# Routed attention and a SiLU layer: a relisted opening, output quarters in any free bank, and one-hot codes scaled on GpSimd and turned by transposing transfers

## The chip, the cores and the metric

The kernel runs on one core of a Trainium2 chip. The core has a matrix engine (TensorE, PE in the profile), a vector engine (VectorE, DVE), an activation engine (ScalarE, ACT), GpSimd (POOL) and SyncE (SP), which here does nothing but issue transfers. Each engine works off its own instructions in order and waits at one until the semaphores that it needs have come. The metric is device time of one execution in microseconds (us); less is better.

## The reference

Four batches of eight heads, 768 tokens, 64 numbers a head. Queries and keys are assigned to the nearest of 16 centroids of their head (by cosine), and a query attends only to the keys of its own cluster. The result passes through a layer with SiLU.

```python
q_assign = np.argmax(np.einsum('bhsd,hcd->bhsc', q_n, c_n), axis=-1)
k_assign = np.argmax(np.einsum('bhsd,hcd->bhsc', k_n, c_n), axis=-1)
mask = q_assign[:, :, :, None] == k_assign[:, :, None, :]
scores = np.where(mask, scale * np.matmul(q, k.transpose(0, 1, 3, 2)), -1000000000.0)
attn = softmax(scores)                      # over the keys
x = matmul(attn, v), heads side by side     # 3072 x 512
h = x @ w_in                                # 3072 x 2048
out = (h * sigmoid(h)) @ w_out              # 3072 x 512, float32
```

## The kernel before

**Masking by matmul.** The mask is not computed as such. Queries and keys lie transposed in a tile `ab` (128 partitions: 64 of the high half of each number in f16, 64 more that at first hold the low halves). The low halves serve the logits against the centroids; then 16 of their partitions (64 to 79) are overwritten with the one-hot code of the row's cluster, scaled by 16384 (`OHV`) and, for keys, shifted by -16384, so that one score matmul gives the product plus 0 for rows of one cluster and a large negative number otherwise. The exponential then does the masking.

**Jobs.** One job prepares one head of one batch: `load` (two transfers on SP's queue, into `raw`, eight buffers), `hi` and `lo` (scale to f16 and the rest, into `hl`), the transpose into `ab` (by PE and an evacuation for batch 0: `tr`, `ev`; by a transposing transfer on SP for the others: `xpose`), `logits`, then on DVE the sum `lsum`, the maximum `mx_n`, and the comparison `ge_n` that writes the one-hot code. The code then has to be turned: `cd_mm` does it with two PE matmuls against the identity, into the right half of a PSUM bank (`psC`), `cd_ev` scales and shifts it on DVE on its way to SBUF (`cd`), and a transfer on SP puts it on partitions 64 to 79 of `ab`. Batch 0 has jobs 0 to 7 for keys and half the queries, and `x0`, `x1` for the other queries of four heads each.

**Steps.** The main work is 192 steps; a step is the scores of one head against two of six key tiles for half of the queries (`qk_mm`: two matmuls of 384 columns into one of two buffers `pS`), and their exponential on ACT (`exp`, 768 columns). Three steps make a head's half. Step 7 + 6n holds attention times v for two heads (`pv`: 36 small matmuls), followed by the normalisation on DVE (`norm`) and a transpose into `xt`, on PE for batch 0 and the last pair, by a transposing transfer (`xn_d`) for the rest. When four such pairs of a half are done, 5 steps later, the half's feed-forward work may start: 16 units A (`unit_a`: four matmuls `ph` of 384 columns, tanh on ACT, one product on DVE into `gt`) and then three output tiles B (`part_b`) of four quarters each (four matmuls `po` of 512 columns); the fourth quarter is followed by an evacuation `ot` and a transfer out.

**Order.** Nothing is scheduled by the compiler: the program is written in the order in which each engine has it. The first 24 steps stand in a list of words (`plan`): `hi0.A` is the high half of job 0 on ACT, `lo`, `tr`, `evk`/`evq`, `L`, `mx`, `ge`, `cm`/`ce` the further parts of a job, `xh`, `xl`, `xp`, `xq`, `xu`, `xw` those of `x0` and `x1`, `qk` and `ex` a step, `pa`/`pb`/`pc` a third of `pv`, `nm` a normalisation, `pt`/`pe` the transpose into `xt`, `vl` and `v` load and conversion of a v, `w` a weight load issued by GpSimd, `j` filler matmuls on zeros, `a` and `e` the first unit A. From step 24 on a loop writes the steps; jobs 8 to 31 have their parts put at fixed steps about p = 32 + 3.5h, 64 + 5h and 104 + 5h for the eight heads h of batches 1, 2 and 3. Units A and quarters B fill what the step leaves: `take` gives them out as long as the estimated PE time of the step (T = 1.46) has room.

**Banks.** PSUM has eight banks: four for the two buffers `pS`, banks 0 to 2 handed out by `bank()` as they come free (`free`), and bank 3, which `part_b` uses for every output tile after the opening.

Of the kernel before, what the change touches and what calls it, by code (L numbers as in the profile page):

```python
# [10 lines left out]
f16 = mybir.dt.float16  # L11
# [5 lines left out]
class Job:  # L17


    def __init__(self, name, srcs, groups, uses):  # L20
        self.name = name
        self.srcs = srcs
        self.groups = groups
        self.uses = uses
        self.n = 3 * len(groups)


@with_exitstack
def kernel(
# [10 lines left out]
    nc = tc.nc  # L40
# [47 lines left out]
    pace = const.tile([1, 1], f16, name="pace")  # L88
    kadd = const.tile([128, 2], f32, name="kadd")
    ohm = [const.tile([128, 2 * HC * 6], f16, name=f"om{n}") for n in range(3)]  # L90


    raws, hls, abs_ = {}, {}, {}
# [104 lines left out]
    def ge_n(job):  # L198
        m = (job.n + 1) // 2
        nn[job.name] = len(nn)  # L200
        mx = mxn.pop(job.name)[:, 0 : 2 * m].rearrange("p (h m) -> p h m", h=2)
        nc.vector.tensor_tensor(
            out=ohv(job), in0=Ls.pop(job.name), in1=mx.unsqueeze(2).to_broadcast([128, 2, HC, m]), op=ALU.is_ge
        )

    def cd_mm(job):
# [314 lines left out]
    def first(op, n, eng, banks):  # L521
# [40 lines left out]
        elif op in ("pa", "pb", "pc"):  # L562
            t = "abc".index(op[1])
            pv(2 * n, 0, banks and banks[0], [(t, 0), (t, 1)])
        elif op in ("px", "py"):
            pv(2 * n, 0, banks and banks[0], [(t, "xy".index(op[1])) for t in range(NM)])
        elif op == "a":
            begun[n] = unit_a_begin(0, 0, n)
        elif op == "e":
            unit_a_end(0, 0, n, begun.pop(n) if n in begun else unit_a_begin(0, 0, n))()  # L570
        elif op == "nm":
            norm(2 * n, 0)
        elif op == "pt":
            xn_t(2 * n, 0, banks[0])
        elif op == "pe":
            xn_ev(2 * n, 0, eng)
        elif op == "xr":
# [24 lines left out]
    plan = """  # L602
        hi0.A lo0 tr0.32 hi2.P j2.1 evk0.D evq0.A c5.01 j2.2 stk hi1.A L0.3 lo2 j1.2 kad xr0
        mx0 tr2.02 hi3.P ge0 j1.1 lo1 j1.1 evk2.A evq2.D ct0.10 hi4.P lo3 vl1 vl0 xr1 L2.2 ctq0 ctk0 tr1.31 mx2 hi5.P
        qk0 evk1.D evq1.A vl2 ex0 tr3.01 ge2 lo4 cm2 hi6.P L1.3 evk3.A ce2.D qk1 vl4 evq3.A mx1 tr4.02 ex1 ge1
        L3.1 hi7.P evk4.D evq4.A qk2 mx3 ct1.02 ex2 ge3 v1 lo5 cm3 ctq1 L4.3 v0 ce3.A ctk1 w0 tr5.01 mx4 v2
        qk3 ge4 evk5.A w1 evq5.D qk4 lo6 cm4 ex3 j2.2 ce4.D vl3 ex4 v4 qk5 lo7 L5.2 ex5 qk6 mx5 tr6.10 ex6 ge5 qk7
        xh0.P evk6.D cm5 ex7 qk8 ce5.D tr7.31 evq6.D ex8 qk9 evk7.D L6.2 vl5 ex9 w2 evq7.D qk10 mx6 v3 L7.0 ex10
        ge6 qk11 cm6 ex11 pa0.3 ce6.D pb0 mx7 qk12 w3 ge7 ex12 v5 qk13 pc0 cm7 ex13 nm0 ce7.D qk14 ex14 xl0 xh1.P qk15 xp0.1 pt0.3 qk16 pe0.D xu0.D xq0.2 xw0.D
        ex15 vl6 w4 ex16 qk17 pa1.0 vl7 xL0.2 qk18 pb1 ex17 w5 xM0 xm0 xg0 qk19 pc1 xc0 ex18 nm1 xe0.D qk20 w6 v6 pa2.1 ex19  # L610
        pt1.0 qk21 pb2 ex20 pe1.D xl1 w7 v7 qk22 pc2 xp1.2 ex21 nm2 xu1.D qk23 xq1.0 px3.3 ex22 pt2.1 xw1.D ex23 w8 pe2.D xL1.2 xM1 xm1 xg1 a0 py3 nm3 xc1 a1 w9 pt3.3 pe3.D xe1.D e0 e1 qk24 ex24 e2
    """.split()
    for word in plan:
        name, *rest = word.split(".")
# [17 lines left out]

    for n in range(10, 12):
        put(25 + 2 * (n - 10), w_load, n, 24 + 2 * (n - 10))
    for i in range(H, B * H):
        b, h = divmod(i, H)
        p = int((32 + 3.5 * h, 64 + 5 * h, 104 + 5 * h)[b - 1]) | 1
        job = jobs[i]
        e = 1 if b == 1 else 2
        put(p - 8 - 2 * (b > 1), load, job)  # L640
        put(p - 6, load_v, i)
        put(p - 3 * e, hi, job)
        put(p - 1 - e, lo, job)
        put(p - e, xpose, job)
# [16 lines left out]
    def take(hold, held):  # L661
# [156 lines left out]
```

## Time and profile before

| what | value |
|---|---|
| time, median of 3 runs | 324.86 us (323.74 to 325.95) |
| the profiled execution: its time / its span | 326.72 us / 324.9 us |
| mean granted clock of TensorE | 0.989 |
| read from / written to main memory | 27.30 MB / 6.29 MB |

The span runs from the first to the last instruction. Shares of busy time are means over stages that differ: the opening with its list (to about 45 us), batch 1's jobs beside the first half's feed-forward work, batches 2 and 3, a stretch without jobs (from about 231 us), and the tail. The page's groups give an operation's mean duration and, behind the bar, the time for which its engine stood idle just before it and what ended that. In the timeline the bracket at the end of a row is such a wait. Matmul ends are modelled, and one begins before its predecessor ends, so distances between starts are the better measure.

### The profile page before, as it was taken

What the parts mean: (1) busy time and instruction counts of PE and PEld (TensorE: products, weight loads), DVE (VectorE), ACT (ScalarE), POOL (GpSimd) and SP (SyncE); (2) the same over time, 40 slices, a digit from 0 to 9 for tenths busy, and PEclk for the clock granted to TensorE, in tenths of its full rate; (3) what the DMA queues carried; (4) which work ended last, traced back from release to release, by engine and by line L of the source; (5) the groups of instructions that cost most, each with busy time, mean ns of one, the idle gap of its engine ahead of it and who ended that gap; (6) DMA issues with size and microseconds to landing.
All of it is one profiled execution on the core that took longest, in us unless ns stands there. A gap on an engine that the chain in (4) does not pass through costs nothing.

```text
span 324.9 us, 7844 instructions
## 1 busy us (share of the span) xinstructions
PE 307.2 (95%) x3173; PEld 191.3 (59%) x3173; DVE 211.7 (65%) x445; ACT 209.4 (64%) x332; POOL 41.0 (13%) x68
## 2 busy tenths in 40 slices
PE   6997999997989999999999999999999999999995
PEld 2665765655556555665566656666566556655644
DVE  5897566779778655987598857893456315632641
ACT  2597649766468665885488656985589648961620
POOL 4884331101000000000010002000000000000000
PEclk9899899999999999999999999999999999999999
DMA  7756999999945686677887567853110111011001
GB/s 218 248 108 132 168 148 253 184 241 206 247 120 135 162 184 186 150 161 132 237 186 185 128 171 210 138 115 83 53 46 12 37 54 46 6 42 46 32 32 68
DMA packets 72613, 43.14 MB, mean 133 GB/s; under 512 B 50016, under 2 KB 68608, under 8 KB 72576
## 3 DMA queue, kind: packets, MB, share of 16 engines
q1 hardware_dynamic: 69024, 38.14, 47.3%
q0 software_dynamic: 3264, 4.20, 8.6%
q8 instruction: 25, 0.41, 0.5%
q10 hardware_dynamic: 288, 0.30, 0.3%
q14 instruction: 12, 0.10, 0.1%
HBM read 27.30 MB, written 6.29 MB: 103 GB/s over the span
## 4 chain that ended last, share of the span: by engine, by line
PE 74%; DVE 14%; ACT 3%; DMA 3%; issue 2%; SPq 2%; POOL 0%; DVEq 0%; ACTq 0%
PE po L430 23%; PE ph L380 20%; PE pS L313 13%; PE pO L330 9%; PE psN L168 3%; DVE hl L120 3%; DVE gt L400 2%; ACT tn L399 2%; DVE ot L437 2%; PE phs L410 2%; ACT P L318 2%; DVE mxn L193 2%; DMA ab<-hl 1%; PE po L782 1%; DVE L L180 1%
## 5 line engine op out<-in xcount | busy, mean ns | idle before, releaser
L318 ACT ACTIVATE P<-pS 128x768 f16<-128x768 f32 x192 | 152.6, 811 | 67.2 <-PE pS L313 67.0
L380 PE MATMUL ph<-xt,win_s 128*128 128x384 f16 x480 | 91.2, 326 | 3.2 <-DVE gt L400 1.7
L313 PE MATMUL pS<-ab 128*128 128x384 f16 x384 | 92.2, 328 | 0.7 <-ACT P L318 0.6
L430 PE MATMUL po<-wout_s,gt 128*128 128x512 f16 x368 | 89.2, 379 | 1.6 <-DVE ot L437 0.9
L400 DVE SCALAR_TENSOR_TENSOR gt<-tn,ph 128x384 f16<-128x384 f32 x120 | 64.0, 551 | 24.3 <-ACT tn L399 23.8
L399 ACT ACTIVATE tn<-ph 128x384 f32<-128x384 f32 x120 | 58.8, 496 | 15.9 <-PE ph L380 11.7
L380 PEld LDWEIGHTS <-win_s 128*128 128x128 f16 x480 | 45.8, 98 | 33.3 <-issue 4.7
L430 PEld LDWEIGHTS <-gt 128*128 128x128 f16 x368 | 34.5, 98 | 37.0 <-issue 3.4
L313 PEld LDWEIGHTS <-ab 128*128 128x128 f16 x384 | 34.7, 98 | 25.5 <-issue 1.7
L330 PEld LDWEIGHTS <-P 128*128 128x128 f16 x1152 | 40.3, 98 | 5.3 <-issue 0.7
L330 PE MATMUL pO<-vt,P 128*128 128x65 f16 x1152 | 41.5, 193 | 0.0
L260 POOL CAST vt<-vn 128x384 f16<-128x384 f32 x32 | 17.0, 533 | 157.5 <-DMA vn<-in_v_dram 127.5
L120 DVE SCALAR_TENSOR_TENSOR hl<-raw,hl 128x768 f16<-128x768 f32 (+3 forms) x35 | 33.9, 972 | 0.4 <-POOL hl L113 0.3
L437 DVE TENSOR_SCALAR ot<-po 128x512 f32<-128x512 f32 x23 | 15.8, 689 | 27.5 <-PE po L430 27.1
L168 PEld LDWEIGHTS <-ab 128*128 128x128 f16 x496 | 18.1, 98 | 5.6 <-DMA ab<-hl 1.5
L180 DVE TENSOR_REDUCE L<-psN 128x192 f32<-128x384 f32 x24 | 13.2, 552 | 11.9 <-PE psN L168 11.9
L168 PE MATMUL psN<-stk,ab 128*128 128x32 f16 (+1 forms) x496 | 19.3, 187 | 1.2 <-DMA ab<-hl 1.1
L342 DVE TENSOR_TENSOR xn<-pO,zr 128x384 f16<-128x384 f32 x32 | 17.8, 557 | 1.1
L340 DVE RECIPROCAL zr<-pO 128x6 f32<-128x6 f32 x32 | 6.2, 194 | 15.7 <-PE pO L330 15.7
L224 DVE TENSOR_SCALAR cd<-psC,kadd 96x256 f16<-96x256 f32 x24 | 11.4, 474 | 6.2 <-PE psC L211 6.0
L113 POOL TENSOR_SCALAR hl<-raw 128x576 f16<-128x576 f32 (+1 forms) x8 | 14.4, 1816 | 2.6 <-DMA raw<-in_q_dram 1.7
L115 DVE TENSOR_SCALAR hl<-raw 128x768 f16<-128x768 f32 x24 | 13.4, 560 | 2.0 <-DMA raw<-in_k_dram 1.9
(68 smaller groups left out, 138.8 us busy)
## 6 DMA issues: line engine op xcount, KB each, us to landing
vn<-in_v_dram SPq DMA_DIRECT2D x32, 192.0 KB, 3.1
raw<-in_k_dram SPq DMA_DIRECT2D x31, 192.0 KB, 3.3
out_dram<-ot SPq DMA_DIRECT2D x23, 256.0 KB, 2.3
raw<-in_q_dram SPq DMA_DIRECT2D x24, 192.0 KB, 2.8
win_s<-in_moe_w_in_dram POOLq DMA_DIRECT2D x8, 256.0 KB, 6.3
wout_s<-in_moe_w_out_dram POOLq DMA_DIRECT2D x4, 512.0 KB, 8.7
ab<-cd SPq DMA_DIRECT2D x26, 48.0 KB, 2.3
raw<-in_q_dram SPq DMA_DIRECT2D x2, 384.0 KB, 5.0
```

Of the source, the lines that this page charges most:

```text
L120: nc.vector.scalar_tensor_tensor(out=hl[:, s, 1, :], in0=raws[job.name][:, s, :], scalar=QS, in1=hl[:, s, 0, :], op0=ALU.mult, op1=ALU.sub ...
L168: nc.tensor.matmul(L[:, n % 2, :, n // 2], ab[:, i, :], stk[:, job.groups[i // 3][0], x : x + w], start=(x == 0), stop=(x + w == 2 * HC),)
L260: nc.gpsimd.tensor_copy(vt[:, :, 0:D], vns.pop(i))
L313: nc.tensor.matmul(pS[:, e, 0:HALF], abs_[kj.name][:, kn, :], rhs, start=True, stop=True)
L318: nc.scalar.activation(out=P, in_=pst.pop(u)[:, :, 0:HALF], func=AF.Exp, bias=0.0, scale=ESC)
L330: nc.tensor.matmul(o[:, (2 * t + h) * VW : (2 * t + h + 1) * VW], Ps[i + h, c, j // 2][:, j % 2, ts(t, 128)], vtb[(i + h) % 13][:, j, 0:VW ...
L342: nc.vector.tensor_tensor(out=xn, in0=ov[:, :, 0:D], in1=zr.unsqueeze(2).to_broadcast([128, 2 * NM, D]), op=ALU.mult)
L380: nc.tensor.matmul(ph[:, 0:HALF], win_s[:, r, ts(fb, 128)], xts[b, c][:, r, :], start=(r == 0), stop=(r == NR - 1))
L399: nc.scalar.activation(out=tn, in_=ph[:, 0:HALF], func=AF.Tanh, bias=0.0, scale=0.5)
L400: nc.vector.scalar_tensor_tensor(out=gt[:, fb, :], in0=tn, scalar=1.0, in1=ph[:, 0:HALF], op0=ALU.add, op1=ALU.mult)
L430: nc.tensor.matmul(po, gts[b, c][:, fc, ts(t, 128)], wout_s[:, fc, :], start=(fc == 0), stop=(fc == NFB - 1))
L437: nc.vector.tensor_scalar(out=ot, in0=po, scalar1=0.5, scalar2=None, op0=ALU.mult)
```

## The change

The opening's list is written anew: the weight loads `w0` to `w7` come earlier, `xl0` moves ahead of `ce7` and `nm0`, `xh1` moves back, job 8 is loaded at the end of the list (`r8`), v 6 and 7 are loaded before it, and the first filler has 13 matmuls and not 11. Loads of batches 1 to 3 are issued earlier. A `part_b` that starts while no unit A is left takes a free bank of 0 to 2 if there is one, and the next tile may follow at once. For jobs 16 to 31 the code is compared into a tile `ohd` with the two parts 128 columns apart, GpSimd scales it in place (`c_scale`, two instructions), a transposing transfer on SP turns it (`c_xpose`), and a second transfer, three steps later, moves it to `ab` (`c_move`); the two matmuls and the evacuation fall away for them.

```diff
+        self.late = name[0] == "h" and int(name[1:]) >= 16
+    ohd = [const.tile([128, 2, 128], f16, name=f"od{n}") for n in range(3)]
     def ohv(job):
         m = (job.n + 1) // 2
+        if job.late:
+            return ohd[nn[job.name] % 3][:, :, 0 : HC * m].rearrange("p h (c m) -> p h c m", m=m)
...
+    def c_scale(job):
+        o = ohv(job)
+        nc.gpsimd.tensor_scalar(out=o[:, :, :, 0:3], in0=o[:, :, :, 0:3], scalar1=OHV, scalar2=None, op0=ALU.mult)
+        nc.gpsimd.tensor_scalar(
+            out=o[:, :, :, 3:6], in0=o[:, :, :, 3:6], scalar1=OHV, scalar2=-OHV, op0=ALU.mult, op1=ALU.add
+        )
+    def c_xpose(job):
+        cd = cds[job.name] = mp.tile([128, 2, 128], f16, name="cdt", bufs=2)
+        nc.sync.dma_start_transpose(cd, ohd[nn[job.name] % 3].rearrange("p h n -> p (h n)"))
+    def c_move(job):
+        cd = cds.pop(job.name)
+        nc.sync.dma_start(
+            abs_[job.name][64 : 64 + HC, :, :].rearrange("p n c -> p (n c)"), cd[0 : 6 * HC].rearrange("p h c -> p (h c)")
+        )
...
-    fill(11)
+    fill(13)
...
-        ge6 qk11 cm6 ex11 pa0.3 ce6.D pb0 mx7 qk12 w3 ge7 ex12 v5 qk13 pc0 cm7 ex13 nm0 ce7.D qk14 ex14 xl0 xh1.P qk15 xp0.1 pt0.3 qk16 pe0.D xu0.D xq0.2 xw0.D
-        ex15 vl6 w4 ex16 qk17 pa1.0 vl7 xL0.2 qk18 pb1 ex17 w5 xM0 xm0 xg0 qk19 pc1 xc0 ex18 nm1 xe0.D qk20 w6 v6 pa2.1 ex19
...
+        ge6 qk11 cm6 ex11 pa0.3 ce6.D pb0 mx7 qk12 w7 ge7 ex12 qk13 pc0 cm7 xl0 ex13 ce7.D vl6 vl7 r8 qk14 nm0 ex14 xp0.1 qk15 xu0.D xq0.2
+        ex15 qk16 xw0.D pt0.3 ex16 pa1.0 pe0.D qk17 xL0.2 ex17 xh1.P pb1 qk18 xM0 xm0 xg0 ex18 pc1 qk19 xc0 nm1 xe0.D v6 v7 ex19
...
+    for od in ohd:
+        put(60, nc.gpsimd.memset, od, 0.0)
     for i in range(H, B * H):
...
-        put(p - 8 - 2 * (b > 1), load, job)
-        put(p - 6, load_v, i)
+        if i > H:
+            put(p - (8 + min(h, 4) if b == 1 else 16), load, job)
+        put(p - (6 if b == 1 else 9), load_v, i)
...
-        put(p + 7, cd_mm, job)
-        put(p + 7, cd_ev, job, "D")
+        if job.late:
+            put(p + 6, c_scale, job)
+            put(p + 6, c_xpose, job)
+            put(p + 9, c_move, job)
+        else:
+            put(p + 7, cd_mm, job)
+            put(p + 7, cd_ev, job, "D")
...
-            f = part_b(*qb.pop(0))
+            f = part_b(*qb.pop(0), None if not qa and free else 3)
             if f:
                 late.append(f)
-                gap = -1
+                gap = -1 if qa else 1
```

More of the change, by code (lines that the diff above doesn't have):

```diff
@@ L203, in ge_n @@
             out=ohv(job), in0=Ls.pop(job.name), in1=mx.unsqueeze(2).to_broadcast([128, 2, HC, m]), op=ALU.is_ge
+        )
[5 more added lines that the diff above has]
+        )
+    cds = {}
+    def c_xpose(job):
[5 more added lines that the diff above has]
+            abs_[job.name][64 : 64 + HC, :, :].rearrange("p n c -> p (n c)"), cd[0 : 6 * HC].rearrange("p h c -> p (h c)")
         )
@@ L576, in first @@
             xn_ev(2 * n, 0, eng)
+        elif op == "r":
+            load(jobs[n])
         elif op == "xr":
@@ L603 @@
         hi0.A lo0 tr0.32 hi2.P j2.1 evk0.D evq0.A c5.01 j2.2 stk hi1.A L0.3 lo2 j1.2 kad xr0
[L604 to L608, printed above, removed]
-        ge6 qk11 cm6 ex11 pa0.3 ce6.D pb0 mx7 qk12 w3 ge7 ex12 v5 qk13 pc0 cm7 ex13 nm0 ce7.D qk14 ex14 xl0 xh1.P qk15 xp0.1 pt0.3 qk16 pe0.D xu0.D xq0.2 xw0.D
-        ex15 vl6 w4 ex16 qk17 pa1.0 vl7 xL0.2 qk18 pb1 ex17 w5 xM0 xm0 xg0 qk19 pc1 xc0 ex18 nm1 xe0.D qk20 w6 v6 pa2.1 ex19
-        pt1.0 qk21 pb2 ex20 pe1.D xl1 w7 v7 qk22 pc2 xp1.2 ex21 nm2 xu1.D qk23 xq1.0 px3.3 ex22 pt2.1 xw1.D ex23 w8 pe2.D xL1.2 xM1 xm1 xg1 a0 py3 nm3 xc1 a1 w9 pt3.3 pe3.D xe1.D e0 e1 qk24 ex24 e2
+        mx0 tr2.02 hi3.P ge0 j1.1 lo1 j1.1 evk2.A evq2.D ct0.10 hi4.P lo3 vl1 vl0 xr1 L2.2 ctq0 ctk0 tr1.31 mx2 hi5.P w0
+        qk0 evk1.D evq1.A vl2 ex0 tr3.01 ge2 lo4 cm2 hi6.P w1 L1.3 evk3.A ce2.D qk1 vl4 evq3.A mx1 tr4.02 ex1 ge1
+        L3.1 hi7.P w2 evk4.D evq4.A qk2 mx3 ct1.02 ex2 ge3 v1 lo5 cm3 ctq1 L4.3 v0 w3 ce3.A ctk1 tr5.01 mx4 v2 vl3
+        qk3 ge4 evk5.A evq5.D qk4 lo6 cm4 w4 ex3 j2.2 ce4.D vl5 ex4 v4 qk5 lo7 L5.2 ex5 qk6 mx5 tr6.10 ex6 ge5 qk7
+        xh0.P w5 evk6.D cm5 ex7 qk8 ce5.D tr7.31 evq6.D ex8 qk9 evk7.D L6.2 v3 ex9 w6 evq7.D qk10 mx6 v5 L7.0 ex10
+        ge6 qk11 cm6 ex11 pa0.3 ce6.D pb0 mx7 qk12 w7 ge7 ex12 qk13 pc0 cm7 xl0 ex13 ce7.D vl6 vl7 r8 qk14 nm0 ex14 xp0.1 qk15 xu0.D xq0.2
+        ex15 qk16 xw0.D pt0.3 ex16 pa1.0 pe0.D qk17 xL0.2 ex17 xh1.P pb1 qk18 xM0 xm0 xg0 ex18 pc1 qk19 xc0 nm1 xe0.D v6 v7 ex19
+        pa2.1 qk20 pt1.0 pb2 ex20 pe1.D qk21 pc2 xl1 ex21 nm2 xp1.2 qk22 xu1.D ex22 xq1.0 px3.3 qk23 xw1.D pt2.1 pe2.D ex23 w8 xL1.2 xM1 py3
+        xm1 xg1 nm3 a0 xc1 pt3.3 a1 w9 pe3.D xe1.D e0 e1 qk24 ex24 e2
     """.split()
```

## The prediction

> **What bounds the kernel.** I read the page first, then busy time by stage, then the chain of waits, then the timeline around each gap of TensorE (PE). The profiled execution took 326.72 us, 324.9 of them span; the median of the three timed runs is 324.86. I work out differences on the span and take them off the median; a profiled run of the new kernel should read about 1.9 us higher.
>
> ```profile
> span 324.9 us, 7844 instructions
> PE 307.2 (95%) x3173; PEld 191.3 (59%) x3173; DVE 211.7 (65%) x445; ACT 209.4 (64%) x332; POOL 41.0 (13%) x68
> ```
>
> ```profile
> 7.90:11.30 3.40, 3.40 (x37) 2.02 (x35) 2.03 (x5) 1.50 (x4) 3.40 (x3) 0.51 0.96 304
> 31.90:35.10 3.20, 3.20 (x28) 2.53 (x27) 1.38 (x3) 0.98 (x2) 3.20 (x7) 0.50 0.98 206
> 0.00:45.50 45.50, 39.04 (x574) 27.25 (x575) 32.69 (x91) 27.14 (x40) 26.27 (x40) 0.92 0.75 170
> 45.50:68.70 23.20, 23.20 (x205) 14.04 (x203) 15.76 (x30) 18.48 (x32) 3.35 (x7) 1.00 1.03 217
> 68.70:85.00 16.30, 13.86 (x172) 8.46 (x171) 13.91 (x30) 9.26 (x12) 2.03 (x4) 1.00 1.02 225
> 116.70:231.00 114.30, 112.00 (x1175) 69.74 (x1173) 85.82 (x173) 78.63 (x124) 7.86 (x14) 1.00 0.67 156
> ```
>
> Columns are stage, length, then PE, PE weight load, DVE, ACT, POOL (busy, instructions), granted clock, DMA share. PE sets the pace nearly everywhere; outside the opening and 68.7 to 85 us it hardly idles. So only three things shorten the run: fewer matmuls, fewer gaps, or a full clock in the two stretches where 0.5 was granted. A busy PE is not PE at its peak, so I price matmuls by distances from start to start:
>
> ```profile
> 251.38 0.33 PE pS L313 x2
> 251.71 0.65 PE ph L380 x4
> 252.36 0.86 PE po L430 x4
> ```
>
> That is 0.33 for a step's two score matmuls, 0.65 for an input-projection unit, 0.86 for an output quarter. A step that takes longer than its matmuls at these prices has lost time.
>
> **Opening (to 45.5 us): -3.0.** Two stalls matter, both followed by half clock.
>
> ```profile
> 1.18 4.13 PE L461 MATMUL junk<-zz 128*128 128x512 f16 x11 [1.18 <-DVE zz L471]
> ```
> ```profile
> 6.90 0.51 PE L143 MATMUL pTk<-ident,hl 128*128 128x128 f16 x6 [1.59 <-DVE hl L120]
> ```
> ```profile
> 10.59 0.32 DVE L193 TENSOR_REDUCE mxn<-psN 128x10 f32<-128x160 f32 x1 [0.99 <-PE psN L168]
> ```
> ```profile
> 78.84 0.52 PE L168 MATMUL psN<-stk,ab 128*128 128x32 f16 x12 [1.13 <-DMA ab<-hl]
> ```
>
> Two more filler matmuls take 2 x 4.13/11 = 0.75 and lie inside the 1.59 wait for the low halves, so they cost nothing; were that wait gone, 0.75. They leave PE 0.84 idle instead of 1.59. The gap of 1.13 at 78.84 left the clock at 1.00, so I expect the dip at 7.9 to 11.3 to go. It is worth 0 (DVE and POOL work beside it) to 1.7 (half of 3.4); I take 0.8, near the 0.99 that DVE waits for the half-speed logits.
>
> ```profile
> 27.98 0.33 DVE L202 TENSOR_TENSOR om<-psN,mxn 128x160 f16<-128x160 f32 x1
> ```
> ```profile
> 30.07 2.13 POOL L113 TENSOR_SCALAR hl<-raw 128x768 f16<-128x768 f32 x1
> 30.08 1.63 DVE L120 SCALAR_TENSOR_TENSOR hl<-raw,hl 128x768 f16<-128x768 f32 x1
> ```
> ```profile
> 31.77 0.82 PE L143 MATMUL pTk<-ident,hl 128*128 128x128 f16 x6 [1.43 <-DVE hl L120]
> ```
> ```profile
> 39.00 0.95 DVE L120 SCALAR_TENSOR_TENSOR hl<-raw,hl 128x768 f16<-128x768 f32 x1
> ```
>
> In the old list `xl0` stands behind `nm0` and `ce7`, beside the GpSimd conversion `xh1`, and takes 1.63; PE waits 1.43 for it. In the new list it follows `ge7` (ending 28.3) and `xh1` comes four steps later: 28.3 + 0.95 to 1.63 = 29.3 to 29.9, while PE came to the transposes that need it at 31.77 - 1.43 = 30.34 and will now come some 0.7 earlier, with two scores and a waiting buffer fewer ahead. Of 1.43 I leave 0.3: -1.1. Then the dip at 31.9 should go too, worth 0 to 1.6; since ACT is busy only 0.98 of 3.20 there, PE sets the time, and I take 1.4. The price of the new order is that `nm0` and the evacuations `xu0`, `xw0` come later on DVE, and weight loads w0 to w2 come ahead of conversions on POOL: 0 to 1.0, taken 0.3. Sum -0.8 - 1.1 - 1.4 + 0.3 = -3.0, between -4.6 and 0.
>
> The Trainium skill ("TensorE: Matmul & The Clock Gate", Part 1) says the clock halves after an idle window of about 3.4 us, a free-running one. The two half-clock stretches are about that long, but each follows only 1.4 to 1.6 us of idle in one piece, so the trace shows a lower threshold; by the page's rule alone neither edit would touch the clock (a rival below).
>
> **Middle (batch 1 jobs, 45.5 to 116.7): -1.3.** Loads go up to four steps earlier on SP's queue, job 8's load goes into the opening. Where DMA is full (share 1.03, 1.02), this moves load traffic and removes none.
>
> ```profile
> 74.33 2.13 SPq L129 DMA_TRANSPOSE ab<-hl  x1
> ```
> ```profile
> 122.46 2.75 PE L430 MATMUL po<-wout_s,gt 128*128 128x512 f16 x12 [0.87 <-DVE ot L437]
> ```
>
> Logits issued in step 48 wait 1.13 (at 78.84) for this transposing transfer. The instruction order of the new program has three output quarters just before these logits instead of one (the new gap rule), 1.7 us of cover that stood behind them: -1.1, and -0.2 for neighbours. Bounds 0 and -2.4, the PE idle in 68.7 to 85 (16.30 - 13.86). DVE is busy 13.91 of 16.30 there and loses no work, so I don't go further.
>
> **Batches 2 and 3 (116.7 on): -2.1.** Sixteen jobs lose two matmuls and one DVE evacuation each.
>
> ```profile
> 133.44 0.49 PE L313 MATMUL pS<-ab 128*128 128x384 f16 x2
> 133.77 0.28 PE L211 MATMUL psC<-ident,om 128*96 128x128 f16 x2
> 134.23 1.46 PE L380 MATMUL ph<-xt,win_s 128*128 128x384 f16 x8 [0.19 <-DVE gt L400]
> 135.53 0.49 PE L313 MATMUL pS<-ab 128*128 128x384 f16 x2
> ```
> ```profile
> 125.37 0.28 PE L211 MATMUL psC<-ident,om 128*96 128x128 f16 x2
> 125.48 1.03 PE L430 MATMUL po<-wout_s,gt 128*128 128x512 f16 x4
> ```
>
> Beside output quarters a pair costs 0.11 (125.37 to 125.48). Beside two units it costs 135.53 - 133.77 - 1.30 = 0.46, as it takes one of three banks and the units wait for one. All 16 lie between 1.8 and 7.4; by the program's order six stand before two units, so 6 x 0.46 + 10 x 0.11 = 3.9 saved.
>
> Output tiles all use bank 3 and wait for its evacuation: 0.87 at 122.46, and smaller ones such as this:
>
> ```profile
> 157.29 0.81 PE L313 MATMUL pS<-ab 128*128 128x384 f16 x4
> 158.24 2.75 PE L430 MATMUL po<-wout_s,gt 128*128 128x512 f16 x12
> ```
>
> Four score matmuls should end at 157.29 + 0.65 = 157.94, so 0.30 is lost. There are about seven such places, some 0.2: 0.87 + 1.8 = 2.7 saved, with a free bank at hand.
>
> Against this the new rule empties the output work earlier, and the new order has bare steps just ahead of each half:
>
> ```profile
> 116.75 0.81 PE L313 MATMUL pS<-ab 128*128 128x384 f16 x4
> ```
> ```profile
> 118.14 0.49 PE L313 MATMUL pS<-ab 128*128 128x384 f16 x2 [0.20 <-ACT P L318]
> ```
>
> Scores have two buffers, so the third bare step waits for ACT: 118.14 - 116.75 = 1.39 for 0.65 of work, 0.74 lost. The new order has four such triples against one: +2.2; twice a bare pair with logits (0.74 - 0.36 = 0.38 each): +0.8; five bursts of four units on three banks, each 0 to 0.46, taken 0.3: +1.5. Together +4.5; -3.9 - 2.7 + 4.5 = -2.1, between -6.6 (none of the new waits) and +0.6 (bursts at 0.46, pairs at 0.11 each).
>
> What takes the removed work's place lies off PE:
>
> ```profile
> L260 POOL CAST vt<-vn 128x384 f16<-128x384 f32 x32 | 17.0, 533 | 157.5 <-DMA vn<-in_v_dram 127.5
> L224 DVE TENSOR_SCALAR cd<-psC,kadd 96x256 f16<-96x256 f32 x24 | 11.4, 474 | 6.2 <-PE psC L211 6.0
> ```
> ```profile
> xt<-xn SPq DMA_TRANSPOSE x23, 2.4
> ```
>
> Two GpSimd scalings of 96 elements are at most 1.7 each (POOL did 768 in 2.13, at 30.07) and at least nothing; I take the nearest row, 0.53. The cover is lead time: codes go to the keys and queries at step 73 + 5h and are first read at 95 + 3h, for the last head eight steps, some 12 us at 254.5 us for 171 steps. Behind a scaling that waits for DVE's comparison stand only conversions of v on POOL, which have time too (they wait 127.5 us for loads). If that cover went, 1.1 + two transfers of 2.4 would show per job. DVE is relieved of 16 x 0.474 = 7.6 us, nothing on PE's path. On SP each job gains one more issue of the kind of `xt<-xn`. The end of the run keeps its work; two output quarters less stand behind the last projection transposes, at most 0.4, taken 0.
>
> Total: -3.0 - 1.3 - 2.1 = -6.4, or 318.5 us.
>
> **Rivals.** *SP's queue (slower).* The new transposing transfer waits at SP for DVE and GpSimd; behind it stand loads, outputs, and `xt<-xn`, which four halves (steps 78, 102, 126, 150) need to start.
>
> ```profile
> SPq L226 <- DVE cd L224: 28.9, 13, 6.4
> ```
> ```profile
> 155.33 1.25 PE L330 MATMUL pO<-vt,P 128*128 128x65 f16 x36
> ```
> ```profile
> 163.38 1.46 PE L380 MATMUL ph<-xt,win_s 128*128 128x384 f16 x8
> ```
>
> From the end of pO (156.58) to the half's first unit are 6.8 us; normalising 0.8, issue 1.2 and landing 2.4 leave 2.4 of slack. If SP stood as long as its longest wait at L226, 6.4, each half would start 4.0 late: 4 x 4.0 = 16, 334.5 us. It turns the sign from 4.0 us of blocking. For it: at steps 121 and 145 the new transfer stands directly ahead of `xt<-xn`. Against: its producers end before that normalisation does.
>
> *Opening only.* The bare steps and bursts cost double the net 2.1 and the middle stays DVE-bound: -3.0, 321.9. For it: output work is conserved, so filler spent early is missing later.
>
> *The clock does not change.* By the page's rule, or because the window falls elsewhere in each run, the 0.8 and 1.4 don't come: 320.7. Against: both dips follow the two longest gaps.
>
> *More comes off.* Opening -4.6, middle -2.4, no new waits late (-6.6): 311.3. Against: the three-step wait is plain arithmetic on two buffers.
>
> **Numbers.** Forecast 0.50; opening only 0.17; clock unchanged 0.10; more 0.10; SP 0.13. A measurement of this kernel tells about 1% from no change: faster means below 321.6, slower above 328.1. Faster: 0.47 + 0.06 + 0.07 + 0.10 = 0.70. Same: 0.03 + 0.11 + 0.03 = 0.17. Slower: 0.13. The range 312 to 325.5 leaves out SP's case and the far end of the good one.
>
> **What would show it.** Right: clock 1.00 in the first 45 us, step 24 some 3 us earlier, no wait for `xl0`, no `DVE ot` ahead of output matmuls, `ACT P` ahead of scores before each half. Wrong: `ph` waiting for the transfer `xt<-xn`, a clock dip at a new place, or longer DVE waits in the opening.

## The result and the profile after

The changed kernel takes 321.60 us (median of 6, 320.87 to 322.76) against 324.81 for the kernel before (6, 323.74 to 325.95): ratio 0.9915, 95% interval 0.9892 to 0.9938. In a second comparison (12 and 25 executions) it was 321.42 against 324.26, 0.9937 [0.9911, 0.9963]. The forecast had 2.0% less and the runs show 0.6 to 0.85%: the sign was right, and half of the gain or more did not come (by the medians it is 3.2 and 2.8 us of the 6.4).

The page of the changed kernel (a profiled execution of 321.51 us): span; busy time, share and instructions by engine; and the granted clock in 40 slices.

```profile
span 319.7 us, 7835 instructions
PE 303.7 (95%) x3143; PEld 187.9 (59%) x3143; DVE 205.1 (64%) x429; ACT 209.5 (66%) x332; POOL 61.6 (19%) x103
PEclk9999999999999999999999999999999999999999
```

DVE has lost 6.6 us of work, POOL has gained 20.6, and the clock is full from 6.75 us on, where its record starts. Line numbers are 24 higher than before from the codes on (`ph` L380 is L404, `po` L430 is L454, `pS` L313 is L337).

Before and after seem to differ by 5.2 us of span, while the medians differ by 3.2. The missing 2 us are the first lesson. Here is another execution of the **kernel before**, unchanged (e1_control), busy time in the two stretches where the first profile had half clock:

```profile
7.90:11.30 3.40, 3.29 (x47) 2.10 (x45) 2.95 (x6) 2.31 (x5) 3.40 (x3) 1.00 0.90 275
31.90:35.10 3.20, 3.03 (x70) 2.42 (x67) 1.60 (x5) 2.60 (x4) 3.20 (x7) 1.00 0.67 139
```

Full clock in both, with nothing changed, as in the changed kernel:

```profile
7.90:11.30 3.40, 3.29 (x46) 2.13 (x44) 3.07 (x6) 2.31 (x5) 3.40 (x3) 1.00 0.97 299
31.90:35.10 3.20, 3.06 (x66) 2.35 (x63) 2.11 (x7) 2.45 (x4) 0.49 (x1) 1.00 0.95 282
```

Of the 107 executions of the kernel before that ran beside the experiments:

| mean granted clock | executions | median us |
|---|---|---|
| 0.999 or 1.000 | 79 | 324.07 |
| 0.996 to 0.998 | 18 | 323.81 |
| below 0.996 | 10 | 325.97 |

The profile of before that I predicted from (0.989, two dips) was one of the rare ones. The mean leaves one thing out: it counts the clock as full until the clock's record starts. Up to there the first fillers follow one another every 0.427 us, and behind it every 0.216 (at 4.71 us in the profile of before). The record starts at 3.9 to 6.8 us in nineteen of the twenty profiles, but at 10.31 in e8_banks (mean 0.998), whose transposes at 7.15 us stand 107 ns apart and not 55. So the table does not count executions whose clock rises late. The changed kernel is not free of dips either: two of the twelve of the second comparison show 0.993 and 0.995 and take 324.86 and 324.50 us.

The table below splits the spans at the starts of step 24 and step 66 (first score matmul):

| profiled execution | start to step 24 | 24 to 66 | 66 to the end |
|---|---|---|---|
| before, as predicted from | 45.53 | 62.65 | 216.8 |
| before (e1_control) | 42.65 | 61.87 | 216.6 |
| changed | 41.59 | 62.96 | 215.2 |
| changed (e5_after_again) | 41.43 | 62.89 | 215.2 |
| e3_opening | 41.60 | 61.99 | 216.8 |
| e4_rest | 43.80 | 62.38 | 215.1 |
| e7_codes | 42.71 | 62.65 | 221.9 |
| e8_banks | 43.94 | 62.74 | 215.7 |
| e11_codes_loads | 43.30 | 62.61 | 215.8 |
| e14_no_banks | 41.76 | 62.96 | 213.6 |
| e17_last_tile_bank3 | 41.59 | 61.16 | 211.8 |

Against the control, the change wins 1.1 in the opening, loses 1.1 in the middle and wins 1.4 after it. That is 1.4 in all and not 3, in part because the control's profiled execution (322.98) lies 0.9 below its own median (323.89), while that of the changed kernel lies at its median. Where a step "loses" time below, it is the distance from the step before, between first score matmuls, less the matmuls in between: 0.1625 for one of `pS` or `ph` and 0.216 for one of `po`, as in the prediction, and, taken from starts in these traces, 1.09 for the 36 of `pO`, 0.06 for one of `psC`, 0.33 for twelve of the logits and 0.33 for six transposes.

The timeline of PE in the changed kernel, at the places where the prediction had named one or time was lost anew: the transposes that need `xl0`, step 15, the logits of step 49, step 66, and the bare triple at step 74.

```profile
28.06 0.51 PE L145 MATMUL pTk<-ident,hl 128*128 128x128 f16 x6 [0.28 <-DVE hl L122]
28.99 0.50 PE L337 MATMUL pS<-ab 128*128 128x384 f16 x2 [0.42 <-DMA ab<-cd]
...
76.23 1.03 PE L454 MATMUL po<-wout_s,gt 128*128 128x512 f16 x4
77.09 0.49 PE L337 MATMUL pS<-ab 128*128 128x384 f16 x2
...
102.76 0.27 PE L235 MATMUL psC<-ident,om 128*96 128x128 f16 x2 [0.33 <-DVE gt L424]
103.69 1.02 PE L454 MATMUL po<-wout_s,gt 128*128 128x512 f16 x4 [0.66 <-DVE gt L424]
...
113.13 0.81 PE L337 MATMUL pS<-ab 128*128 128x384 f16 x4
114.51 0.49 PE L337 MATMUL pS<-ab 128*128 128x384 f16 x2 [0.57 <-ACT P L342]
```

The wait for `xl0` is down to 0.28, close to the 0.3 that was left for it, but step 15 now waits for a code; the logits wait no more; at step 66 an output tile waits for a unit's product; and 114.51 - 113.13 - 0.65 = 0.73 is lost at the triple, as forecast (0.74).

### The profile page after: what moved, and what is told of

It reads as the page before. It is cut to its first block, busy times and chain, and to the rows that moved or that the text cites. A ratio compares the mean times of both kernels' runs of the same rounds, so it can differ in the third digit from the quotient of the medians.

```text
span 319.7 us, 7835 instructions
## 1 busy us (share of the span) xinstructions
PE 303.7 (95%) x3143; PEld 187.9 (59%) x3143; DVE 205.1 (64%) x429; ACT 209.5 (66%) x332; POOL 61.6 (19%) x103
## 4 chain that ended last, share of the span: by engine, by line
PE 77%; DVE 10%; DMA 6%; ACT 4%; issue 1%; POOL 0%; DVEq 0%; ACTq 0%
PE po L454 24%; PE ph L404 20%; PE pS L337 15%; PE pO L354 10%; ACT P L342 3%; PE psN L170 3%; DVE hl L122 2%; DMA ab<-hl 2%; DMA ab<-cd 2%; PE phs L434 2%; DVE gt L424 1%; DVE mxn L197 1%; PE po L817 1%; DVE L L182 1%; DMA craw<-in_centroids_dram 1%
## 5 line engine op out<-in xcount | busy, mean ns | idle before, releaser
L337 PE MATMUL pS<-ab 128*128 128x384 f16 x384 | 91.8, 326 | 3.5 <-ACT P L342 2.9
L404 PE MATMUL ph<-xt,win_s 128*128 128x384 f16 x480 | 90.7, 326 | 3.2 <-DVE gt L424 1.3
L454 PE MATMUL po<-wout_s,gt 128*128 128x512 f16 x368 | 89.7, 379 | 0.7 <-DVE gt L424 0.7
L404 PEld LDWEIGHTS <-win_s 128*128 128x128 f16 x480 | 46.1, 98 | 34.6 <-issue 4.7
L454 PEld LDWEIGHTS <-gt 128*128 128x128 f16 x368 | 34.8, 98 | 35.1 <-issue 0.8
L337 PEld LDWEIGHTS <-ab 128*128 128x128 f16 x384 | 34.6, 98 | 29.8 <-issue 4.8
L354 PEld LDWEIGHTS <-P 128*128 128x128 f16 x1152 | 39.6, 97 | 4.8 <-DVE gt L424 0.7
L284 POOL CAST vt<-vn 128x384 f16<-128x384 f32 x32 | 23.0, 731 | 53.6 <-DMA vn<-in_v_dram 45.2
L213 POOL TENSOR_SCALAR od<-od 128x96 f16<-128x96 f16 x16 | 9.3, 580 | 97.5 <-DVE od L206 91.6
L115 POOL TENSOR_SCALAR hl<-raw 128x576 f16<-128x576 f32 (+1 forms) x8 | 15.6, 1962 | 1.9 <-DMA raw<-in_q_dram 1.9
L117 DVE TENSOR_SCALAR hl<-raw 128x768 f16<-128x768 f32 x24 | 13.8, 575 | 0.0
```

The costliest lines, as they stand in the source:

```text
L284: nc.gpsimd.tensor_copy(vt[:, :, 0:D], vns.pop(i))
L337: nc.tensor.matmul(pS[:, e, 0:HALF], abs_[kj.name][:, kn, :], rhs, start=True, stop=True)
L354: nc.tensor.matmul(o[:, (2 * t + h) * VW : (2 * t + h + 1) * VW], Ps[i + h, c, j // 2][:, j % 2, ts(t, 128)], vtb[(i + h) % 13][:, j, 0:VW ...
L404: nc.tensor.matmul(ph[:, 0:HALF], win_s[:, r, ts(fb, 128)], xts[b, c][:, r, :], start=(r == 0), stop=(r == NR - 1))
L454: nc.tensor.matmul(po, gts[b, c][:, fc, ts(t, 128)], wout_s[:, fc, :], start=(fc == 0), stop=(fc == NFB - 1))
```

## The experiments

**e1_control**: the kernel before, unchanged.

> The kernel before, unchanged, run again. Theory A (the clock dips of the opening depend on where a free-running window falls): the mean granted clock differs between executions, some show 1.00 or one dip (about 0.995) and are about 1 us shorter per dip missing; the median lies about 1 to 2 us under the profiled 326.72. Rival B (the dips come in every execution, since the idle gaps are fixed by data arrival): all executions show 0.989 and spread by less than 1 us.

323.89 us, 1.000 [0.9975, 1.0024]. The mean clock differs between executions, 0.994 to 1.000 in these twelve, as theory A had it. The profile is the one quoted above: step 0 at 12.73 us, not 13.98.

**e2_filler**: the two fillers alone.

```diff
-    fill(11)
+    fill(13)
```

> The kernel before with 13 instead of 11 matmuls in the first filler, nothing else. Theory A: the first dip goes where it came, so the median drops by 0 to 0.8 us and the second dip stays in some executions. Rival B: 0.8 us less in every execution. Rival C (the dip costs nothing, DVE and GpSimd set the pace there): under 0.2 us.

324.12 us, 1.0003 [0.9982, 1.0024]: no gain that these runs can tell, and by the interval at most 0.6 us. What the fillers do can be seen all the same. In the seven profiles with 11 fillers the wait for the first low halves was as long as 1.71 us, and three ran at half clock at 8 us: before and e16_before_pace by a dip, e8_banks by its late rise. Their step 0 begins at 13.77 to 14.16 us, that of the other four at 12.57 to 12.73. In the thirteen with 13 fillers the wait was at most 1.08, and none ran at half clock there.

**e3_opening**: the new list, 13 fillers and job 8's early load; the rest as before.

> The kernel before with the new opening list alone (with the 13 fillers and the early load of job 8; later loads, codes and output banks as before). If the changed kernel's gain comes from the opening: about -3 us at the median and step 24 near 41.6 us in the profile; if half of the opening's 3.9 us in the profile was the phase of the clock: -2 us. If step 24 comes early and the end does not, the middle stage gave it back.

323.21 us, 0.998 [0.9957, 1.0003]: 0.5 us at the median, and by the interval between 1.4 less and no change. In the profile step 24 starts at 41.60, just as in the whole change, and the later stages are those of before. So the list gives what it gives by itself.

**e4_rest**: the whole change with the old list and its 11 fillers.

> The kernel before with everything but the opening: earlier loads of batches 1 to 3, GpSimd codes and transposing transfers for batches 2 and 3, output quarters in any free bank. From the row by row comparison of the two traces: -1.7 us from step 72 on, and 0 to +0.3 before it, so -1.5 us at the median. Rival: the parts are not additive (the opening's gain lets the middle wait for DVE instead), then this alone gives -2.5 or more.

322.50 us, 0.9954 [0.9933, 0.9976]: most of the gain lies behind the opening.

**e5_after_again**: the changed kernel once more; its time stands above.

> The changed kernel again, on the same chip as the next three. If the two halves measured alone add up (-0.5 for the opening, -1.3 for the rest): about 0.994 of the kernel before. If its first measurement (0.9915) holds, 0.8 us more than the parts comes from their meeting. Clock 1.00 in all executions, as in its first six, against some at 0.994 to 0.999 for the kernel before.

**e6_pace**: a smaller time per step, so that work for PE is given out more slowly and lasts until the next half.

```diff
-    T = 1.46
+    T = 1.42
```

> The changed kernel with the estimated step time T at 1.42 instead of 1.46, so that the loop gives filler out more slowly. In the program's order no three steps stand bare any more after batch 1 and no unit burst of four. Theory (the bare steps and bursts are a cost of this change: 4 x 0.74 + 2 x 0.41 + about 0.4 for bursts): 2.5 to 3.5 us under the changed kernel. Rival (PE's total is what counts and the waits reappear elsewhere): within 0.5 us of it.

322.80 us, 0.9958 [0.9938, 0.9978], no better. Up to step 125 it was 3.3 us ahead of the changed kernel by time lost (13.8 against 17.1): the triples were gone. Then nearly every step of the next half lost 0.35:

```profile
199.12 0.81 PE L404 MATMUL ph<-xt,win_s 128*128 128x384 f16 x4 [0.49 <-DVE gt L424]
199.76 0.49 PE L337 MATMUL pS<-ab 128*128 128x384 f16 x2
200.09 0.81 PE L404 MATMUL ph<-xt,win_s 128*128 128x384 f16 x4
201.09 0.81 PE L404 MATMUL ph<-xt,win_s 128*128 128x384 f16 x4 [0.19 <-DVE gt L424]
201.74 0.49 PE L337 MATMUL pS<-ab 128*128 128x384 f16 x2
```

About every second unit waits for the product of the one before the last, as if there were two banks and not three.

**e7_codes**: the codes alone on the kernel before; head loads stay at p - 10.

```diff
-        put(p + 7, cd_mm, job)
-        put(p + 7, cd_ev, job, "D")
+        if job.late:
+            put(p + 6, c_scale, job)
+            put(p + 6, c_xpose, job)
+            put(p + 9, c_move, job)
+        else:
+            put(p + 7, cd_mm, job)
+            put(p + 7, cd_ev, job, "D")
```

> The kernel before with the GpSimd codes and transposing transfers for batches 2 and 3 alone. Theory: the pairs of matmuls and their bank waits go, 3.9 us by the prediction's sum, less one bare triple that loses its psC pair and stays as long; new bare steps because the loop's credit counts 0.11 less per job: net -2 to -3 us. Rival (SP's queue gives it back): xt<-xn waits at half starts and under -1.

327.72 us, 1.0114 [1.0086, 1.0142]: 1.1% **slower** than before. This is the rival of SP's queue, and the trace shows its chain. First SP's issues, then DVE, then PE:

```profile
208.80 0.50 SPq L102 DMA_DIRECT2D raw<-in_q_dram  x1
209.34 0.43 SPq L102 DMA_DIRECT2D raw<-in_k_dram  x1
209.88 1.20 SPq L222 DMA_TRANSPOSE cdt<-od  x1
```
```profile
212.74 0.56 DVE L117 TENSOR_SCALAR hl<-raw 128x768 f16<-128x768 f32 x1 [2.36 <-DMA raw<-in_k_dram]
213.22 0.19 DVE L364 RECIPROCAL zr<-pO 128x6 f32<-128x6 f32 x1
213.44 0.56 DVE L366 TENSOR_TENSOR xn<-pO,zr 128x384 f16<-128x384 f32 x1
```
```profile
214.06 1.46 PE L404 MATMUL ph<-xt,win_s 128*128 128x384 f16 x4 [2.65 <-DVE xn L366]
```

A head's loads are issued at 208.8, its conversion on DVE waits 2.36 for them, the normalisation queued behind the conversion frees the bank for which PE waits 2.65, and in this execution the clock halves for 3.41 us on top (329.08 us, 0.993; the other five of this kernel, at 0.999 or 1.000, take 326.51 to 328.75). In all, by the groups of DVE instructions (idle time behind the bar), the conversion waits 13.2 us here and never in e11, where the loads come earlier:

```profile
L117 DVE TENSOR_SCALAR hl<-raw 128x768 f16<-128x768 f32 x24 | 13.4, 558 | 13.2 <-DMA raw<-in_k_dram 13.2
```
```profile
L117 DVE TENSOR_SCALAR hl<-raw 128x768 f16<-128x768 f32 x24 | 13.6, 567 | 0.0
```

**e11_codes_loads**: e7 with the change's loads (second fence above).

```diff
-        put(p - 8 - 2 * (b > 1), load, job)
-        put(p - 6, load_v, i)
+        put(p - (8 + min(h, 4) if b == 1 else 16), load, job)
+        put(p - (6 if b == 1 else 9), load_v, i)
```

> The kernel before with the codes of batches 2 and 3 on GpSimd and SP, and with the earlier loads, without the new opening and without the new banks: e7_codes and the earlier loads. Theory: the loss of e7_codes comes from head loads that stand on SP's queue behind the two new transfers and reach the conversion hl<-raw too late (DVE waits 2.36 us for raw at 212.7 us in e7_codes, and the pair's normalisation, on which PE waits 2.65, stands behind it). With the loads issued six steps earlier that wait goes, and the time is 321.5 to 323.5, at or below the kernel before, since 32 matmul pairs' worth of psC (some 1.9 us) is gone. Rival: the transfers themselves (cdt and ab landing beside full DMA) are what costs, and the time stays above 326.

321.68 us, 0.9921 [0.9890, 0.9952]. The loads turn 1.1% slower into 0.8% faster: the prediction named this cover ("the cover is lead time") but looked for it at the codes; it was needed at the loads behind them. And this much is nearly the gain of the whole change. The earlier loads without the codes were not run: the same conversion waits 1.9 us in the control, so a part of this gain may be theirs.

**e8_banks**: the bank rule and the new gap alone.

```diff
-            f = part_b(*qb.pop(0))
+            f = part_b(*qb.pop(0), None if not qa and free else 3)
...
-                gap = -1
+                gap = -1 if qa else 1
```

> The kernel before with output quarters in any free bank and the new gap alone. Theory: 2.7 us of waits for ot go, two bare triples (0.74 each) and the first quarter's wait for a bank whose product is still being read (0.8 at step 66) come: 0 to -0.5 us net. Rival: as predicted, -2.7 without the price of the bare steps.

322.59 us, 0.994 [0.9913, 0.9966]: a gain of 1.7 on the kernel before, by medians. So codes with loads take 2.7 off, banks 1.7, the opening 0.5; yet all together only 2.8 to 3.2.

**e14_no_banks**: the whole change without those two lines.

> The changed kernel without its rule for banks (every output tile in bank 3 and the old gap): new opening, earlier loads, codes. Theory: of the bank rule's saving (2.7 for waits on the evacuation, 1.1 at step 50, as predicted) nothing is left in the whole change, because with the pairs of psC gone it brings the bare triples and bursts and the wait at step 66; then this kernel is as fast as the changed one or faster, 320.3 to 321.6. Rival, as the prediction had it: the rule is worth 2.7 + 1.3 less 1.5 + 1.5 + 0.8, some 1.5 us, and without it the time is 322.5 to 323.5.

320.45 us, 0.9882 [0.9852, 0.9913], about 1.0 below the changed kernel's 321.42 and 321.60. Inside the change the rule **costs** time. The intervals of this one pair overlap, but two further pairs differ by the rule alone and go the same way: e4_rest (0.9954) against e11_codes_loads (0.9921), and e12_cd4 (321.57 us) against e18_no_banks_cd4 (320.59). From step 67 on, steps that lose over 0.25 us in three profiles:

```
e8_banks      74: 0.62  79: 0.63  84: 0.35  104: 0.26  108: 0.34  114: 0.34  134: 0.34  138: 0.34  175: 0.74
changed       74: 0.74  79: 0.74  104: 0.88  109: 0.28  122: 0.41  128: 0.36  146: 0.41  170: 0.74  175: 0.74
e14_no_banks  74: 0.74  96: 0.34  101 121 125 145 149 168 173: 0.29 each  136: 0.45  170: 0.74
```

The seven of 0.29 are the waits for bank 3, 2.0 us. The rule removes them and pays 0.74 at 79 and 175 and 0.3 to 0.9 at 104, 109, 122, 128 and 146. The pacing counts the pairs of `psC` as work: in the order of e8_banks' instructions the steps 120, 144 and 168 have an output quarter each. Without the pairs the quarters are handed out earlier (in the changed kernel two in step 143 and not one), those three steps are bare, and 122, 128, 146 and 170 lose 1.9. The group of score matmuls shows more waiting for the exponential, first of the changed kernel, then of e14 (idle time behind the bar):

```profile
L337 PE MATMUL pS<-ab 128*128 128x384 f16 x384 | 91.8, 326 | 3.5 <-ACT P L342 2.9 <-DMA ab<-cd 0.4
```
```profile
L337 PE MATMUL pS<-ab 128*128 128x384 f16 x384 | 90.8, 326 | 2.6 <-ACT P L342 1.4 <-DMA ab<-cd 1.1
```

e14 also settles steps 50 and 66. Its logits wait again and its output tile does not:

```profile
74.75 0.52 PE L170 MATMUL psN<-stk,ab 128*128 128x32 f16 x12 [0.73 <-DMA ab<-hl]
...
103.75 0.27 PE L235 MATMUL psC<-ident,om 128*96 128x128 f16 x2 [0.33 <-DVE gt L424]
103.86 1.02 PE L454 MATMUL po<-wout_s,gt 128*128 128x512 f16 x4
```

At step 66 the "free" bank is free in the order of the program, while its last reader, a unit's product on DVE, has not run yet; in bank 3 the tile starts without a wait. That is 1.30 lost against 0.48.

**e10_bank3_only**: output tiles begun without units alternate between bank 3 and a free one (T = 1.46).

```diff
-            f = part_b(*qb.pop(0), None if not qa and free else 3)
+            q0 = qb.pop(0)
+            if q0[3] == 0:
+                alt = not qa and not alt
+            f = part_b(*q0, None if not qa and not alt and free else 3)
```

> The changed kernel with the alternation of bank 3 and a free bank alone (T stays 1.46). Theory: the first output tile at step 66 no longer waits 0.66 for the product of the last unit, 0.8 us less than the changed kernel, 320.3 to 321.0; the bare triples (0.74 at steps 74, 79, 170, 175) stay. Rival: with two tiles of three in bank 3, waits for its evacuation come back (0.2 to 0.9 each) and the time is that of the changed kernel or up to 1 us above.

321.94 us, 0.9915 [0.9884, 0.9946]: a miss. With three tiles a half the alternation changes its parity, so the tile of step 66 still took a free bank, and the step still lost 1.30.

**e9_pace_b3**: the same with T = 1.42.

> The changed kernel with T = 1.42 instead of 1.46, and with the output tiles begun while no unit A is left alternating between bank 3 (first) and a free bank. My theory of the slow second half of e6_pace: at 191 us three quarters of an output tile lie in one of banks 0 to 2 when the next half's units begin, its fourth quarter comes only at 212.8 us, so the units have two banks and lose 0.35 in nearly every step. If so, the step-by-step losses between steps 126 and 163 (7.1 us in e6_pace, 1.2 in the changed kernel) fall below 2, the wait of the first output tile at step 66 (0.82) goes, and the time is 316 to 318.5 us. Rival 1: the units lose because T = 1.42 gives them out too closely for DVE and ACT, whatever the bank: the losses from 126 on stay near 7 and the time is 321.5 to 323. Rival 2: work saved before step 125 is only lent, and the later stage gives it back as bare steps: 320 to 321.5.

320.93 us, 0.9877 [0.9841, 0.9912]. (Between steps 126 and 163 e6_pace had lost 7.9, not the 7.1 of the theory.) Steps 125 to 139 still lose 5.3 (changed kernel: 0.6), but steps 150 to 163 fall from 2.35 in e6_pace to 0.01: one of two halves mended, which fits the bank.

**e13_banks_chosen**: T = 1.42, a free bank for the first and the last tile of a half.

```diff
+            f = part_b(*q0, None if not qa and free and q0[2] != 1 and q0[:3] != (0, 1, 0) else 3)
```

> e9_pace_b3 with another choice of banks: T = 1.42, and an output tile begun while no unit A is left takes a free bank only if it is not the middle one of its half's three (the one that lies unfinished when the next half's units begin at step 127) and not the first of the second half (step 66). Theory: in e9_pace_b3 the middle tile of the half before step 127 still lay in one of banks 0 to 2, because the alternation changes its parity with three tiles a half; the losses between steps 126 and 139 (5.3 us there, 0.6 in the changed kernel) fall to 1.5 or less, the loss at step 66 from 1.30 to 0.48, and the time is 316.3 to 318 us. Rival: the units of that half lose by T alone: its losses stay at 4 or more and the time stays at 320 to 321.

324.61 us, 0.9997 [0.9976, 1.0019]: a bad miss, and the telling one. I had taken the wrong tile. In the order of the program 11 of 12 quarters are out when step 126's units start, so it is the *last* tile that lies unfinished. Here it was in a free bank in both halves, and both lost: 5.5 and 2.3 us. The twelfth quarters come in steps 139 and 163, and just there the losses end. At step 66 it was, with this T, the sixteenth unit that took the occupied bank.

**e17_last_tile_bank3**: T = 1.42, a free bank for the middle tile only.

```diff
+            q0 = qb.pop(0)
+            f = part_b(*q0, None if not qa and free and q0[2] == 1 else 3)
```

> e13_banks_chosen with the free bank for the middle output tile of a half only: the first and the last lie in bank 3 (T = 1.42). By the program's order the tile that lies unfinished from step 127 on is the last of the three (11 of its half's 12 quarters are out), not the middle one as e13_banks_chosen assumed: it had the last tile in a free bank in both halves and lost 0.35 a step in both (126 to 139 and 151 to 163), e9_pace_b3 in one half only, the one whose last tile was free. Theory: with the last tile in bank 3 both halves lose what the changed kernel loses: steps 126 to 139 from 5.3 (e9_pace_b3) to 2 or less, 151 to 163 to 0.3, and the time is 317 to 319. Rival: the loss in e13_banks_chosen and e9_pace_b3 is of DVE's order of work at that pace, and the banks only coincide: it stays at 4 or more in one of the halves, 321 or above.

317.48 us, 0.9789 [0.9765, 0.9812]: 2.1% below the kernel before, and about 4 us below the changed one. Steps 125 to 139 lose 1.8, steps 150 to 163 0.01. Groups of PE in this kernel: output quarters wait for nothing, scores for no exponential.

```profile
L337 PE MATMUL pS<-ab 128*128 128x384 f16 x384 | 92.9, 326 | 0.7 <-DMA ab<-cd 0.4
L454 PE MATMUL po<-wout_s,gt 128*128 128x512 f16 x368 | 90.9, 379 | 0.0
```

What is left at step 126 are two transfers that come late:

```profile
187.84 0.52 PE L170 MATMUL psN<-stk,ab 128*128 128x32 f16 x12 [0.58 <-DMA ab<-hl]
...
191.89 0.97 PE L404 MATMUL ph<-xt,win_s 128*128 128x384 f16 x5 [0.67 <-DMA xt<-xn]
```

**e15_no_banks_pace**: e14 with T = 1.42. **e16_before_pace**: the kernel before with T = 1.42.

> e14_no_banks with T = 1.42. Theory: the output work then reaches to the next half and no step is bare, without any tile in banks 0 to 2: the bare triple at step 74 and the one at 170 go (1.5 us), nothing is lost from 126 on by banks, and the time is 318.5 to 320. Rival: the quarters left late all lie in bank 3 and wait for its evacuation, which gives the 1.5 back: 320.5 to 322.

> The kernel before with T = 1.42 alone. Theory: there the pairs of psC and the last bare steps are what pace buys; only the triple at step 74 goes (0.6 us): 323.3 to 324. Rival: the pace is itself the gain seen in e9_pace_b3, and the kernel before falls by 2 or more, to 322 or less.

320.94 us, 0.9911 [0.9878, 0.9945], and 323.69 us, 0.9976 [0.9953, 1.0000]. The pace alone is worth little, before or without free banks, and with the changed kernel's own choice of bank it gave 322.80 us (e6_pace): at this pace the choice of bank is what makes e17's gain. The same choice with T = 1.46 was not run, so that it needs the pace as well is argued from the bare steps and not shown. (The median of e15 is no better than that of e14, though its profiled execution, its fastest, loses less up to step 191, 17.1 against 19.1; its tail from step 191 on is 34.0 us against 31.1, as work is left over for it.)

**e12_cd4** and **e18_no_banks_cd4**: four buffers for `cd` in the changed kernel and in e14.

```diff
-        cd = mp.tile([6 * HC, 256], f16, name="cd", bufs=2)
+        cd = mp.tile([6 * HC, 256], f16, name="cd", bufs=4)
```

> The changed kernel with four buffers for the turned code cd instead of two. In the new opening the comparison's evacuation into cd waits 1.17 for the transfer ab<-cd that still reads its buffer, and the scores of step 15 wait 0.55 for the code. Theory A: the buffer is the cause; then both waits go, step 24 begins 0.3 to 0.6 us earlier (41.0 to 41.3 us instead of 41.6) and the time falls by as much. Theory B: the transfers themselves have become slow (4.6 to 5.1 us to landing instead of 3.3 to 3.9) because weight loads now run beside them; then DVE no longer waits but the scores still do, and step 24 stays at 41.5 to 41.7.

> e14_no_banks with four buffers for cd. Theory: the two small edits add up, as e12_cd4 began step 24 0.4 us earlier counted from step 0 (5.1 lost there in the changed kernel, 4.7 with four buffers): 319.8 to 320.3. Rival: the wait for the transfer moves to the next use and the time stays at 320.4 to 320.8.

321.57 us, 0.9913 [0.9878, 0.9948], and 320.59 us, 0.9890 [0.9870, 0.9911]: no difference that these runs can tell. DVE at this place in the changed kernel and in e12:

```profile
29.04 0.48 DVE L248 TENSOR_SCALAR cd<-psN,kadd 80x256 f16<-80x256 f32 x1 [1.04 <-DMA ab<-cd]
```
```profile
27.20 0.47 DVE L248 TENSOR_SCALAR cd<-psN,kadd 80x256 f16<-80x256 f32 x1
```

DVE's wait is gone, as theory A had it, but the scores of step 15 still lose 0.86 (1.04 in the changed kernel; 1.59 in e18_no_banks_cd4, which has four buffers too), as B had it. Issues and median landing times of the five-cluster codes in the control and in the changed kernel:

```profile
ab<-cd SPq DMA_DIRECT2D x6, 40.0 KB, 3.9
```
```profile
ab<-cd SPq DMA_DIRECT2D x6, 40.0 KB, 4.6
```

The transfers take 0.7 longer; that the weight loads beside them are the reason was not tried apart.

## Why the forecast was right in sign and wrong in size

**Opening, -3.0: -0.5 came at the median of e3_opening, about -1.2 between profiles.** This is the first of two steps that failed. The terms -0.8 and -1.4 for two clock dips, and the 1.1 of the 1.43 wait for `xl0`, were sizes of one execution, taken off a median of others. The mechanism of the first dip is real: with half clock there step 0 begins 1.0 us or more later (13.77 to 14.16 against 12.73 in the control). But with e2_filler's 13 matmuls, behind which no profile shows it, the median does not move (at most 0.6 by the interval), so the 0.8 was not there to save; how many executions have half clock there stays open, as the mean clock does not count a late rise. The second dip came in one of the eight profiles with the old list. The wait for `xl0` is 0.74 in the control, and step 15's wait for its code took part of its place. Over the profiles without half clock at 8 us, step 24 begins at 43.0 on average with the old list (five: 42.41 to 43.80) and at 41.7 with the new (twelve: 40.81 to 43.49). The rival "clock does not change" named this term.

**Middle, -1.3: about +0.7 came** (62.26 on average in the two profiles of the kernel before, 62.93 in the two of the changed one). The step as put was right: the logits of step 49 lost 0.6 to 1.6 in ten profiles with the old rule for banks (mean 1.1) and 0.02 in all ten with the new one. What failed, the second step, was "DVE loses no work, so I don't go further": I listed no new wait there. The free bank at step 66 gave back 0.82 (1.30 lost and not 0.48), and the other steps from 44 to 55 lose 2.7 and 3.0 in the changed kernel against 2.3 in both profiles of the kernel before, among them a wait of 0.32 of the logits for `ab<-hl` at step 46. Those vary between executions (step 46: 0.52 and 0.15 in two of the same kernel) and are not traced further.

**Batches 2 and 3, -2.1: -1.4 came**, by the steps that were given. The codes: -3.9 forecast, 216.6 - 213.6 = -3.0 from step 66 on (e14 against the control; 32 x 0.06 = 1.9 of it the matmuls themselves). In e11's profile, its slowest execution (323.48 us, median 321.68), it is only -0.8; units wait 1.4 for `xt<-xn` there: the SP rival's wait, nearly all of it in one place of one execution. The bank rule: -2.7 + 4.5 = +1.8 forecast, 215.2 - 213.6 = +1.6 measured (changed kernel against e14), with the triples at 74, 79, 170 and 175 and the pairs at 122 and 146 where the order of the program had them. Its waits for bank 3 were 7 x 0.29 = 2.0, not 2.7. The term should have been read for what it said: a part of the change that costs 1.8 us here, less the 1.1 that the middle's term credited to it. (The stage's upper bound, put at +0.6, adds up to +0.8 from the terms named for it.)

**GpSimd and SP.** In the group of GpSimd instructions the two scalings take 580 and 298 ns for the 0.53 taken, and the turned transfer lands in 2.4, as taken. The SP rival did not decide the change, but only because the loads were moved with it: without that its sign comes true (e7_codes, +3.5 us, by the loads, which it had named among what stands behind, and not by `xt<-xn`, by which it was priced).

```profile
L213 POOL TENSOR_SCALAR od<-od 128x96 f16<-128x96 f16 x16 | 9.3, 580 | 97.5 <-DVE od L206 91.6 <-DMA xt<-xn 5.9
L214 POOL TENSOR_SCALAR od<-od 128x96 f16<-128x96 f16 x16 | 4.8, 298 | 0.0
```

The stages add to -1.2 + 0.7 - 1.4 = -1.9, and the measured medians differ by 2.8 and 3.2. The rest is some 0.9 to 1.3. The control's profiled execution lies 0.9 below its median, which may be most of it; no experiment places it in a stage.

## What to carry to other kernels

Before a stall or a clock dip of a profile is taken off a median, compare that profile's own time and mean clock with those of the other executions: what happens in a few of them cannot be saved in the median. When a kernel hands out filler by a pace, removing real work is also removing filler, so set the pace anew with every such change, and look at which buffer the unfinished piece of work holds when the next stage starts. A part whose worth depends on another has to be priced together with it: the codes cost time without the early loads, and the rule for banks pays on the kernel before and costs time beside the new codes and loads.

## What the runs showed of the hardware

In 20 profiled executions, up to 300 us, the granted clock was halved four times after it had risen, each time for 3.41 us. In the clock's record it changes only at whole multiples of 3.41 us from the record's start (before: 4.42, 7.83, 11.24, 31.72 and 35.13 us). In the 3.41 us ahead of the four changes to half PE stood idle for 1.82 and 1.68 (before), 1.94 (e16_before_pace) and 2.35 us (e7_codes). In all other stretches of that grid it stood idle for at most 1.64 us (e4_rest, 4.88 to 8.29), then 1.46 (e18_no_banks_cd4), and the clock stayed full. Busy time and clock just behind the change in e7_codes:

```profile
213.80:217.20 3.40, 3.14 (x10) 1.49 (x11) 2.53 (x6) 1.30 (x2) 1.58 (x4) 0.50 0.71 149
```

So here it was the idle time of PE summed over such a stretch that told the two apart, at some 1.65 us, about half of it, and where a gap falls on the grid, which differs between executions, decides whether it is halved. The ends of matmuls are modelled, so the second digit is not certain. The Trainium skill ("TensorE: Matmul & The Clock Gate", Part 1) speaks of an idle window of about 3.4 us: the length agrees, the need for a whole idle window does not.
